# Clearing the raw weight blocks: other planning rules and new early due times

## The chip, the cores and the metric

The kernel runs on one core of one Trainium2 chip. The metric is the device time of one execution in microseconds (us). TensorE is called PE here, its weight loads PEld, VectorE DVE, ScalarE ACT, GpSimd POOL and the queue of transfers SP, as in the profile.

## The reference

The program chains three layers; everything is float32.

```python
# 1. a scan per batch (4) and head (8), 768 steps, state 48 x 48, complex decay
S_re, S_im = ar*S_re - ai*S_im + k[t] (x) v[t],  ar*S_im + ai*S_re
y[t] = q[t] @ S_re
# 2. x = y as 3072 tokens x 384;  rms norm, then a dense gated layer of width 1536
xn = x / sqrt(mean(x*x) + 1e-6) * rms_g
x  = (silu(xn @ w_gate) * (xn @ w_val)) @ w_out
# 3. 8 experts of width 1024, each token goes to its best one
e   = argmax(x @ w_gate2);  p = softmax(x @ w_gate2)[e]
out = p * (relu(x @ w1[e]) @ w2[e])
```

## The kernel before

The 3072 tokens are cut into 12 units of 256 tokens, each of two chunks of 128. A unit goes through three stages. `elem(u)` makes the decayed q and k of the scan with logarithms, exponentials, sines and running sums on ACT, DVE and POOL, and spreads them over partitions with transfers (tile QK). `attention(u)` calls `chunk` twice: scores, masking, products with v and with the state, and at the end the rms norm of each token (the root) and the split of the result into a high part xh and a low part xl. `dense(u)` runs 12 features of 128 columns: `stage1` is 18 matmuls, `stage2` 6, with a tanh and a few DVE steps between them. After unit 11 the experts follow.

The dense weights arrive as 64-bit floats, in 12 blocks: w00 to w03 of the gate, w10 to w13 of the value, wo0 to wo3 of the output. Features 0 to 2 need w00, w10 and wo0, features 3 to 5 need w01, w11 and wo1, and so on. `convert` turns a block into a high and a low part: three transfers into the block's own place, then in one of the raw buffers a memset (line 418), `top` (lines 395 and 397), `join` (line 401), `high` (lines 406 and 408), and `low` (line 411; for w00 and wo0 PE does it, lines 430 and 431, and ACT copies it, line 434). There are two raw buffers for all 12 blocks (NRAW=2), and `logit_columns` borrows them too. A raw buffer is given to a block when the first of its steps that touches it, the memset, is put in order.

The order of all instructions is made when the program is built, by `Plan.issue`. Each step has a list of engines with an estimated cost, the steps that it must follow (worked out from what it reads, r, and writes, w), and a due time. At each turn the planner finds the earliest time at which any step could begin, and among the steps that could begin then on that engine it takes the one with the smallest due time. So due times are priorities, and no real times. A step with `lock=True` is planned as using the port that DVE and POOL share: two locked steps on DVE or POOL are never planned at the same time. Each engine then runs its own list in that order, and waits only for the data that an instruction really touches.

A filler (`keep_warm`, line 1388) is planned on PE only where no other PE step could begin, and only up to W1=107.43 us of planned time; it multiplies a converted block into a buffer that nobody reads.

The due times that matter here: `due_moe(0, 3*g)` is 771.62 + 14.31 g, a block w{n}{g} is due at that + CG + C{n}{g}, a block wo{g} at that + CO + C2{g}. `due_elem(0)` is E0 + EU0 and `due_elem(1)` is 771.62 + E1 + EU1. `due_att(0)` is A0, with AC0 more for the second chunk; `due_att(1)` is 771.62 + A1 + AU1. Inside convert, the transfers of a block beyond the fifth in order of creation (w00, w10, wo0, w01, w11, wo1, w02, w12, wo2, w03, w13, wo3) are planned only after the `top` of the block five before it (AHEAD=5).

Of the kernel before, what the change touches and what calls it, by code (L numbers as in the profile page):

```python
# [27 lines left out]
          AF.Tanh: ("exp", "arctan", "sin")}  # L28
TABLE_LOAD = 1.3

TUNE = dict(T0=771.62, PER=649.53, FT=4.77, A0=-422.97, A1=-431.72, A2=-35.5, E0=-1137.13, E1=236.14, E2=1375.6,
            E3=785.18, CG=483.05, CO=263.88, LC=-203.35, NRAW=2, AHEAD=5, DH=547.2, FI=-16.42, RP=-1165.15, TOL=0,
            S2L=28.66, NS=3, NH=3, HOP=0.2, W1=107.43, ATP=2, PA0=0, PA1=0.08, PE0=0, PE1=0.24, RG=1, LB=-24.77,
            EB=-56.74, RB=6.57, HB=-60.28, MB=-8.8, TB=10.11, AX=1, EE=-12.66, EL=7.32, BEG=0.7, DL=2, FN=8,
            FF=15, LW=1, LO=1, C00=-926.96, C01=-266.61, C02=382.08, C03=-259.36, C10=-529.22, C11=-373.75, C12=-583.49,
            C13=1773.0, C20=-587.24, C21=781.76, C22=1957.05, C23=2500.91, C30=583.92, C31=-599.84, C32=-15.96, C33=-423.27,
            AU1=282.87, AU2=-63.05, AU3=-787.85, AU4=-777.43, EU0=224.54, EU1=294.16, EU2=16.71, EU3=-24.77,
            EU4=41.45, EU5=43.43, AC=73.5, AC0=4.7)
HOP = TUNE["HOP"]


# [92 lines left out]
class Plan:  # L134
# [5 lines left out]
    def add(self, engs, fn, r=(), w=(), due=0.0, table=None, lag=0.0, after=(), size=0, span=(0.0, math.inf), pull=0.0, lock=False):  # L140

        s = Step()
        s.size, s.span, s.pull, s.lock = size, span, pull, lock
        s.engs = [engs] if isinstance(engs, tuple) else engs
        s.fn, s.due, s.table, s.lag = fn, due, table, lag
        s.next, s.end, s.seq = [], None, len(self.steps)
        deps = {id(a): a for a in after}
        bufs = {}  # L150
        for writes, items in ((False, r), (True, w)):
            for x in items:
                b, part = x if isinstance(x, tuple) else (x, None)
                bufs[id(b)] = b
                for p, (wr, rd) in b.last.items():
                    if p == part or p is None or part is None:
                        for d in ([wr] if wr else []) + (rd if writes else []):
                            deps[id(d)] = d
        for writes, items in ((False, r), (True, w)):
            for x in items:  # L160
                b, part = x if isinstance(x, tuple) else (x, None)
                if writes:
                    if part is None:
                        b.last.clear()
                    b.last[part] = (s, [])
                else:
                    b.last.setdefault(part, (None, []))[1].append(s)
        deps.pop(id(s), None)
        s.bufs = list(bufs.values())
        for b in s.bufs:  # L170
            b.users += 1
        s.deps = list(deps.values())
        s.wait = len(s.deps)
        for d in s.deps:
            d.next.append(s)
        self.steps.append(s)
        return s
# [73 lines left out]
def kernel(ctx, tc, qT, kT, reT, imT, v, wg, wv, wo, rg, w2g, w1, w2, out):  # L251
    nc = tc.nc
    V, A, G, TE, SP = nc.vector, nc.scalar, nc.gpsimd, nc.tensor, nc.sync
# [123 lines left out]
    paces = []  # L377
# [3 lines left out]
    def convert(name, src, n, due, by_pe):  # L381

        place = Slots(left, name, [P, KD, n, 2], I32)
        st, raw, w = Buf(place), Buf(k_raw), Buf(place, shape=[P, KD, 2, n], dtype=F32R)
        N = KD * WB

        def halves():
            return st.t.rearrange("p k n t -> p k (n t)").bitcast(U16)

        def top(e):  # L390

            h = halves().bitcast(BF16).rearrange("p k (n t) -> p k n t", t=4)[:, :, 1:WB + 1, 0]
            o = raw.t.bitcast(F16).rearrange("p k (n t) -> p k n t", t=2)[:, :, :, 1]
            if e is A:
                e.activation(o, h, AF.Copy)
            else:
                e.tensor_scalar(out=o, in0=h, scalar1=1.0, scalar2=1.0, op0=ALU.mult, op1=ALU.mult)

        def join(e):
            ri = raw.t.bitcast(I32)  # L400
            e.scalar_tensor_tensor(out=ri, in0=st.t[:, :, :WB, 1], scalar=13, in1=ri,
                                   op0=ALU.logical_shift_right, op1=ALU.bitwise_or)

        def high(e):
            if e is A:
                e.activation(w.t[:, :, 0, :WB], raw.t, AF.Copy)
            else:
                e.tensor_scalar(out=w.t[:, :, 0, :WB], in0=raw.t, scalar1=1.0, scalar2=1.0, op0=ALU.mult, op1=ALU.mult)

        def low(e):  # L410
            e.tensor_tensor(out=w.t[:, :, 1, :WB], in0=raw.t, in1=w.t[:, :, 0, :WB], op=ALU.subtract)

        for k in range(KD):
            dma(lambda e, k=k: e.dma_start(halves()[:, k, 1:1 + 4 * WB], src[k * P:(k + 1) * P]),
                P * WB * 8, w=[(st, f"k{k}")], due=due, after=paces[-AHEAD:][:1] if len(paces) >= AHEAD else ())
        light = [(A, act(N)), (G, 0.08 + N * 1.04e-3), (V, dve(N / 2), TUNE["RB"])]
        pairs = [(st, f"k{k}") for k in range(KD)]
        add((G, 0.08 + N * 0.96e-3), lambda e: e.memset(raw.t, 0.0), w=[raw], due=due - 2, lock=True)
        paces.append(add(light, top, r=pairs, w=[raw], due=due, lock=True))
        add((V, dve(N)), join, r=pairs + [raw], w=[raw], due=due, lock=True)  # L420
        add(light, high, r=[raw], w=[(w, 0)], due=due, lock=True)
        if not by_pe:
            add([(G, pool2(N)), (V, dve(N), TUNE["LB"])], low, r=[raw, (w, 0)], w=[(w, 1)], due=due, lock=True)
            return w

        for k in range(KD):
            ps = bank(P, WB)

            def left_over(e, k=k, ps=ps):
                TE.matmul(ps.t, lhsT=ident, rhs=raw.t[:, k, :], start=True, stop=False)  # L430
                TE.matmul(ps.t, lhsT=NEGR.t, rhs=w.t[:, k, 0, :WB], start=False, stop=True)

            add((TE, mm(WB, 4) + mmr(WB)), left_over, r=[raw, (w, 0), NEGR], w=[ps], due=due)
            add((A, act(WB)), lambda e, k=k, ps=ps: e.activation(w.t[:, k, 1, :WB], ps.t, AF.Copy),
                r=[ps], w=[(w, f"l{k}")], due=due)
        return w
# [212 lines left out]
    def chunk(u, c, QK, vt, xh, xl, first, last):  # L649
# [143 lines left out]
                fn(e)  # L793

        if u < TUNE["RG"]:
            at((V, 0.19 * len(tiny_ops)), together, r=[rs], w=[rs])
        else:
            for fn in tiny_ops:
                at((V, 0.1), fn, r=[rs], w=[rs])
        at((A, act(DM)), lambda e: e.activation(wide(y.t), flat(), AF.Copy, scale=rs.t[:, 1:2]), r=[yp, rs], w=[y])  # L800
        xt = bank(P, KD, C)

# [754 lines left out]
```

## Time and profile before

| what | us |
|---|---|
| median of 3 runs | 936.32 (935.12 to 940.16) |
| the profiled execution: its time | 936.97 |
| the profiled execution: span, first to last instruction | 935.3 |
| PE busy | 896.5 (96% of the span) |
| DVE busy | 613.2 (66%) |
| ACT busy | 518.0 (55%) |
| POOL busy | 181.6 (19%) |
| mean granted clock of PE, as a share of full speed | 0.992 |

Busy times are those of the profiled execution. A busy PE need not do useful work: the filler counts as busy. Times of instructions count from the start of the span. A line number is that of the kernel before; the engine name stands ahead of it, and `out<-in` names what an instruction writes and reads.

### The profile page before, as it was taken

What the parts mean: (1) busy time and instruction counts of PE and PEld (TensorE: products, weight loads), DVE (VectorE), ACT (ScalarE), POOL (GpSimd) and SP (SyncE); (2) the same over time, 40 slices, a digit from 0 to 9 for tenths busy, and PEclk for the clock granted to TensorE, in tenths of its full rate; (3) what the DMA queues carried; (4) which work ended last, traced back from release to release, by engine and by line L of the source; (5) the groups of instructions that cost most, each with busy time, mean ns of one, the idle gap of its engine ahead of it and who ended that gap; (6) DMA issues with size and microseconds to landing.
All of it is one profiled execution on the core that took longest, in us unless ns stands there. A gap on an engine that the chain in (4) does not pass through costs nothing.

```text
span 935.3 us, 17743 instructions
## 1 busy us (share of the span) xinstructions
PE 896.5 (96%) x6747; PEld 863.5 (92%) x6747; DVE 613.2 (66%) x1528; ACT 518.0 (55%) x996; POOL 181.6 (19%) x226
## 2 busy tenths in 40 slices
PE   2699999999999999999999999999999999999996
PEld 2689999999999999999999999999989989999996
DVE  5699867778777768686868777546566642545510
ACT  7787876675655656655656565424426433544421
POOL 3232302010111010110201020101242532222121
PEclk9899999999999999999999999999999999999999
DMA  9955233423333140605050421102346753545200
GB/s 331 292 196 140 65 78 82 102 83 77 95 61 94 45 127 18 154 18 154 17 137 19 92 80 40 48 1 66 93 122 200 219 144 111 151 129 182 91 23 23
DMA packets 68363, 98.12 MB, mean 105 GB/s; under 512 B 16038, under 2 KB 49257, under 8 KB 68276
## 3 DMA queue, kind: packets, MB, share of 16 engines
q1 hardware_dynamic: 57316, 86.61, 32.9%
q0 software_dynamic: 10688, 9.95, 3.9%
q8 instruction: 54, 0.88, 0.4%
q10 hardware_dynamic: 272, 0.40, 0.1%
q14 instruction: 33, 0.27, 0.1%
HBM read 68.19 MB, written 10.15 MB: 84 GB/s over the span
## 4 chain that ended last, share of the span: by engine, by line
PE 68%; DVE 11%; issue 8%; DMA 5%; ACT 5%; POOL 2%; SPq 0%; POOLq 0%; DVEq 0%; ACTq 0%
PE m L850 25%; PE a L873 15%; PE a L1317 7%; PE m L1299 7%; PE t L680 4%; PE t L720 3%; DVE ee L541 2%; PE t L724 1%; DMA out_dram<-eo,idx 1%; PE t L698 1%; POOL out_dram L1325 1%; DMA QK<-qk 1%; DMA rawb<-in_w_dram 1%; DVE re L576 1%; DVE rs L785 1%
## 5 line engine op out<-in xcount | busy, mean ns | idle before, releaser
L850 PE MATMUL m<-xh,w 128*128 128x256 f32 x1728 | 276.6, 285 | 1.1 <-DVE s L862 0.6
L850 PEld LDWEIGHTS m<-xh,w 128*128 128x128 f32 x1728 | 234.6, 188 | 5.7 <-issue 3.4
L873 PE MATMUL a<-wo,hh 128*128 128x392 f32 (+1 forms) x576 | 151.8, 345 | 0.0
L850 PE MATMUL m<-xl,w 128*128 128x256 f32 x864 | 149.1, 281 | 0.0
L850 PEld LDWEIGHTS m<-xl,w 128*128 128x128 f32 x864 | 122.3, 188 | 0.0
L873 PEld LDWEIGHTS a<-wo,hh 128*128 128x128 f32 x576 | 100.5, 188 | 0.7 <-issue 0.7
L873 PE MATMUL a<-wo,hl 128*128 128x392 f32 (+1 forms) x288 | 98.3, 341 | 1.7 <-DVE hl L867 1.7
L865 ACT ACTIVATE hh<-s 128x256 fp32r<-128x256 f32 x144 | 59.5, 415 | 72.9 <-PE a L873 45.7
L857 ACT ACTIVATE s<-m 128x256 f32<-128x256 f32 x144 | 54.6, 380 | 77.8 <-PE m L850 40.1
L867 DVE TENSOR_TENSOR hl<-s,hh 128x256 fp32r<-128x256 f32 x144 | 66.6, 467 | 29.4 <-ACT hh L865 28.7
L859 DVE SCALAR_TENSOR_TENSOR s<-s,m 128x256 f32<-128x256 f32 x144 | 59.4, 413 | 21.3 <-ACT s L857 21.1
L1325 POOL DMA_INDIRECT out_dram<-eo,idx x28 | 37.2, 1330 | 157.7 <-ACT eo L1323 91.2
L1308 DVE SCALAR_TENSOR_TENSOR ehl<-m,ehh 128x384 fp32r<-128x384 f32 (+6 forms) x64 | 35.2, 555 | 44.6 <-ACT ehh L1306 44.0
L862 DVE SCALAR_TENSOR_TENSOR s<-s,m 128x256 f32<-128x256 f32 x144 | 59.6, 415 | 2.1
L1323 ACT ACTIVATE eo<-a,eg 114x384 f32<-114x384 f32 (+5 forms) x28 | 16.3, 582 | 74.9 <-PE a L1317 60.6
L873 PEld LDWEIGHTS a<-wo,hl 128*128 128x128 f32 x288 | 54.1, 188 | 2.3 <-DVE hl L867 2.3
L1306 ACT ACTIVATE ehh<-m 128x384 fp32r<-128x384 f32 (+6 forms) x64 | 31.2, 491 | 44.8 <-PE m L1299 41.7
L720 PE MATMUL t<-AK,vt 128*64 128x224 f32 (+3 forms) x384 | 49.6, 346 | 0.5 <-ACT raw L465 0.3
L680 PE MATMUL t<-QK 96*128 96x128 f32 x384 | 48.1, 276 | 0.3 <-DMA QK<-ee 0.3
L680 PEld LDWEIGHTS t<-QK 96*128 96x128 f32 x384 | 46.3, 192 | 1.3 <-issue 0.8
L948 POOL DMA_INDIRECT slots<-tid,sl x24 | 25.0, 1043 | 115.7 <-DVE cnt L943 111.8
L690 DVE TENSOR_TENSOR AK<-t,mask 128x512 f32<-128x512 f32 x40 | 26.9, 686 | 21.3 <-PE t L680 21.1
(290 smaller groups left out, 1853.0 us busy)
## 6 DMA issues: line engine op xcount, KB each, us to landing
rawb<-in_w_dram SPq DMA_DIRECT2D x21, 512.0 KB
rawb<-in_w_dram SPq DMA_DIRECT2D x28, 384.0 KB
QK<-qk SPq DMA_DIRECT2D x24, 290.2 KB
QK<-ee SPq DMA_DIRECT2D x24, 290.2 KB
re<-in_a_re_dram SPq DMA_DIRECT2D x12, 384.0 KB
im<-in_a_im_dram SPq DMA_DIRECT2D x12, 384.0 KB
qk<-in_q_dram SPq DMA_DIRECT2D x12, 384.0 KB
qk<-in_k_dram SPq DMA_DIRECT2D x12, 384.0 KB
```

What stands on the lines that cost most here:

```text
L680: TE.matmul(sc.t[:, i, :], lhsT=K(4 * g + i), rhs=Q(4 * g + i), start=True, stop=True)
L720: TE.matmul(yt.t[64 * n:64 * n + d, i, :n_], lhsT=vs[:, o:o + d], rhs=ak.t[:, 2 * i + n, :n_], start=True, stop=first)
L850: TE.matmul(ps.t[:, i, :], lhsT=W1[i, g].t[:, k, part, fs], rhs=x.t[:, k, :], start=(n == 0), stop=(n == 3 * KD - 1))
L857: add((A, act(U)), lambda e: e.activation(s.t, ps.t[:, 0, :], AF.Tanh, scale=0.5), r=[ps], w=[s], due=dh, table=AF.Tanh)
L859: add((V, dve(U)), lambda e: e.scalar_tensor_tensor(out=s.t, in0=s.t, scalar=1.0, in1=ps.t[:, 0, :], op0=ALU.add, op1=ALU.mult), r=[s, ps] ...
L862: add((V, dve(U)), lambda e: e.scalar_tensor_tensor(out=s.t, in0=s.t, scalar=0.5, in1=ps.t[:, 1, :], op0=ALU.mult, op1=ALU.mult), r=[s, ps ...
L865: add((A, act(U)), lambda e: e.activation(hh.t, s.t, AF.Copy), r=[s], w=[hh], due=dh)
L867: lambda e: e.tensor_tensor(out=hl.t, in0=s.t, in1=hh.t, op=ALU.subtract), r=[s, hh], w=[hl], due=dh, lock=True)
L873: TE.matmul(acc[t].t[:, :wide], lhsT=h.t[:, ts_], rhs=WO[g].t[:, k3, part, :wide], start=(f == 0 and n == 0), stop=(f == KF - 1 and n == 2))
L1299: TE.matmul(ps.t, lhsT=w.t[:, k, fs], rhs=y.t[:, k, :], start=(i == 0), stop=(i == 3 * KD - 1))
L1317: TE.matmul(po.t, lhsT=h.t[:, f, js], rhs=w.t[:, f, :], start=(f == 0 and i == 0), stop=(f == KF2 - 1 and i == 2))
L1325: add((G, 1.05), lambda e, o=o, j=j: e.indirect_dma_start(out=outs[(x + j) % len(outs)], out_offset=bass.IndirectOffsetOnAxis(ap=at(j), ax ...
```

## The change

Three things are edited. In `convert`, the memset of the raw buffer is no longer planned as a user of the shared port (`lock=True` is gone), and from the third block created on the planner must put it after the landing of the first of the block's three transfers (`r=pairs[:1]`). In `chunk`, the root is planned as a user of the shared port: all its instructions together for unit 0, the third one alone (line 785) for the other units, where each of them is a step of its own. And 33 constants of `TUNE` have new values, all of them due times; the numbers of buffers, the costs of the steps and what is computed stay.

```diff
--- before.py
+++ after.py
@@ -28,14 +28,14 @@
           AF.Tanh: ("exp", "arctan", "sin")}
 TABLE_LOAD = 1.3
 
-TUNE = dict(T0=771.62, PER=649.53, FT=4.77, A0=-422.97, A1=-431.72, A2=-35.5, E0=-1137.13, E1=236.14, E2=1375.6,
-            E3=785.18, CG=483.05, CO=263.88, LC=-203.35, NRAW=2, AHEAD=5, DH=547.2, FI=-16.42, RP=-1165.15, TOL=0,
+TUNE = dict(T0=771.62, PER=649.53, FT=4.77, A0=-208.38, A1=-534.31, A2=-35.5, E0=-913.69, E1=-117.22, E2=1310.91,
+            E3=785.18, CG=782.95, CO=398.33, LC=-594.82, NRAW=2, AHEAD=5, DH=547.2, FI=-16.42, RP=-439.99, TOL=0,
             S2L=28.66, NS=3, NH=3, HOP=0.2, W1=107.43, ATP=2, PA0=0, PA1=0.08, PE0=0, PE1=0.24, RG=1, LB=-24.77,
             EB=-56.74, RB=6.57, HB=-60.28, MB=-8.8, TB=10.11, AX=1, EE=-12.66, EL=7.32, BEG=0.7, DL=2, FN=8,
-            FF=15, LW=1, LO=1, C00=-926.96, C01=-266.61, C02=382.08, C03=-259.36, C10=-529.22, C11=-373.75, C12=-583.49,
-            C13=1773.0, C20=-587.24, C21=781.76, C22=1957.05, C23=2500.91, C30=583.92, C31=-599.84, C32=-15.96, C33=-423.27,
-            AU1=282.87, AU2=-63.05, AU3=-787.85, AU4=-777.43, EU0=224.54, EU1=294.16, EU2=16.71, EU3=-24.77,
-            EU4=41.45, EU5=43.43, AC=73.5, AC0=4.7)
+            FF=15, LW=1, LO=1, C00=-812.72, C01=-145.33, C02=-151.56, C03=-365.19, C10=-584.52, C11=-760.4, C12=-636.1,
+            C13=1713.57, C20=-538.76, C21=451.62, C22=2534.06, C23=2073.79, C30=271.16, C31=-476.58, C32=605.07, C33=-1214.84,
+            AU1=394.45, AU2=-1136.16, AU3=-1119.07, AU4=-815.88, EU0=32.96, EU1=286.28, EU2=521.23, EU3=-24.77,
+            EU4=41.45, EU5=43.43, AC=73.5, AC0=830.33)
 HOP = TUNE["HOP"]
 
 
@@ -415,7 +415,7 @@
                 P * WB * 8, w=[(st, f"k{k}")], due=due, after=paces[-AHEAD:][:1] if len(paces) >= AHEAD else ())
         light = [(A, act(N)), (G, 0.08 + N * 1.04e-3), (V, dve(N / 2), TUNE["RB"])]
         pairs = [(st, f"k{k}") for k in range(KD)]
-        add((G, 0.08 + N * 0.96e-3), lambda e: e.memset(raw.t, 0.0), w=[raw], due=due - 2, lock=True)
+        add((G, 0.08 + N * 0.96e-3), lambda e: e.memset(raw.t, 0.0), r=pairs[:1] if len(paces) > 1 else [], w=[raw], due=due - 2)
         paces.append(add(light, top, r=pairs, w=[raw], due=due, lock=True))
         add((V, dve(N)), join, r=pairs + [raw], w=[raw], due=due, lock=True)
         add(light, high, r=[raw], w=[(w, 0)], due=due, lock=True)
@@ -793,10 +793,10 @@
                 fn(e)
 
         if u < TUNE["RG"]:
-            at((V, 0.19 * len(tiny_ops)), together, r=[rs], w=[rs])
+            at((V, 0.19 * len(tiny_ops)), together, r=[rs], w=[rs], lock=True)
         else:
-            for fn in tiny_ops:
-                at((V, 0.1), fn, r=[rs], w=[rs])
+            for i, fn in enumerate(tiny_ops):
+                at((V, 0.1), fn, r=[rs], w=[rs], lock=i == 2)
         at((A, act(DM)), lambda e: e.activation(wide(y.t), flat(), AF.Copy, scale=rs.t[:, 1:2]), r=[yp, rs], w=[y])
         xt = bank(P, KD, C)
 
```

## Rows read from the trace of the kernel before

**Rows 1.** Three stretches: length, then busy PE, PEld, DVE, ACT, POOL, clock, DMA, GB/s.
```profile
0.00:60.00 60.00, 34.94 (x231) 28.79 (x232) 39.63 (x60) 46.37 (x66) 21.05 (x50) 0.94 0.95 313
60.00:84.00 24.00, 23.95 (x174) 23.68 (x173) 22.70 (x49) 19.82 (x32) 5.82 (x6) 1.00 0.25 83
84.00:130.00 46.00, 45.50 (x399) 42.83 (x398) 38.51 (x89) 37.23 (x68) 9.92 (x14) 1.00 0.32 79
```

**Rows 2.** Filler matmuls, groups by line: first 0 to 130, then 66 to 130.
```profile
L1388 PE MATMUL a<-w,identr 128*128 128x384 f32 x120 | 24.5, 358 | 5.3 <-ACT w L406 5.2
...
L1388 PE MATMUL a<-w,identr 128*128 128x384 f32 x28 | 5.5, 341 | 0.0
```

**Rows 3.** Chain that ended last, 0 to 130: start us, us, what.
```profile
30.57 8.35 DMA QK<-qk
...
38.93 3.08 DMA QK<-ee
...
52.54 1.27 DVE raw L401
...
54.09 1.69 DVE rs L785
...
57.12 1.27 DVE w L411
...
64.05 1.25 DVE raw L401
65.30 0.78 DVE xl L815 x3
...
76.09 6.40 PE m L850 x54
...
83.89 3.15 PE a L873 x18
```

**Rows 4.** Stretches of 10 us; the last two columns are DMA share and GB/s.
```profile
10.00:20.00 10.00, 3.27 (x6) 1.82 (x7) 8.17 (x16) 7.70 (x9) 1.27 (x1) 1.00 1.03 396
30.00:40.00 10.00, 4.79 (x26) 4.65 (x25) 6.77 (x6) 7.49 (x9) 1.18 (x2) 0.67 1.07 222
```

**Rows 5.** Timeline of POOL: start us, us, instruction, idle before and releaser.
```profile
20.94 1.15 POOL L418 MEMSET raw<- 128x1152 f32 x1 [0.27 <-PE t L430]
...
53.94 1.81 POOL L546 TENSOR_TENSOR im<-im,re 128x768 f32<-128x768 f32 x1 [2.30 <-ACT re L533]
```

**Rows 6.** Timeline of ACT, conversion steps of weight blocks.
```profile
30.79 1.50 ACT L395 ACTIVATE raw<-w 128x1152 f16<-128x1152 bf16 x1 [0.52 <-POOL raw L418]
32.88 1.50 ACT L395 ACTIVATE raw<-w 128x1152 f16<-128x1152 bf16 x1 [0.59 <-DMA w<-in_wv_dram]
...
35.72 2.20 ACT L406 ACTIVATE w<-raw 128x1152 fp32r<-128x1152 f32 x2
```

**Rows 7.** Timeline of DVE, 15 to 23 us.
```profile
15.32 1.36 DVE L401 SCALAR_TENSOR_TENSOR raw<-w,raw 128x1152 int32<-128x1152 int32 x1 [1.14 <-ACT raw L395]
16.60 2.03 DVE L554 TENSOR_TENSOR ee<-ee 128x256 f32<-128x256 f32 x3
...
20.51 0.58 DVE L585 TENSOR_SCALAR ta<-re 128x768 f32<-128x768 f32 x1
21.12 1.38 DVE L587 TENSOR_SCALAR ta<-ta 128x768 f32<-128x768 f32 x1
```

**Rows 8.** Line 785, the root: nanoseconds minimum, median, maximum of its instructions.
```profile
L785 DVE TENSOR_TENSOR rs<-magic,rs x24: 125/159/1805, 54.1 to 632.4; 128x1 int32<-128x1 int32 x24
```

**Rows 9.** DMA issues by line in 0 to 60: count, KB each.
```profile
w<-in_wg_dram SPq DMA_DIRECT2D x12, 384.0 KB
```

**Rows 10.** Timeline of DVE: first and last of unit 1's rest, 14 instructions.
```profile
66.19 1.09 DVE L554 TENSOR_TENSOR ee<-ee 128x256 f32<-128x256 f32 x3
...
82.86 1.82 DVE L613 TENSOR_TENSOR ee<-ee,re 128x768 f32<-128x768 f32 x2
```

**Rows 11.** The page's costliest groups: one of the dense stage's vector steps.
```profile
L859 DVE SCALAR_TENSOR_TENSOR s<-s,m 128x256 f32<-128x256 f32 x144 | 59.4, 413 | 21.3 <-ACT s L857 21.1
```

## Prediction

> **What bounds the kernel now.** I read the busy times by stretch first. From 84 us on PE hardly idles: 45.50 of 46 us are busy [rows 1]. In the first 60 us it is busy for only 34.94 us [rows 1], and the filler takes 24.5 us of the first 130, the last 5.5 of them after 66 us [rows 2]. So what the kernel loses it loses before about 84 us: some 25 us idle and 24.5 us of filler. The change alters nothing that PE must compute, so it can win or lose only by when useful PE work is ready there, and by new gaps later.
>
> The chain of waits says what ready depends on. The spread of unit 0 (QK) lands at 38.9 and 42.0 us [rows 3], behind a transfer queue that moves 396 GB/s between 10 and 20 us and is still full from 30 to 40 [rows 4]. From 52 to 66 us the chain runs through DVE: root, conversion steps of weight blocks, and the last piece of unit 0's xl, which ends at 66.08 [rows 3]. Dense work starts right after it. DVE is busy for 22.70 of the 24 us from 60 to 84 [rows 1]: it is the engine that unlocks PE work there.
>
> **The change part by part.**
>
> *The raw buffers.* Before, the memset has nothing to wait for, so the planner hands a free raw buffer to the block with the smallest due time, landed or not. The due times of before give 327.7 for w00, 448.3 for wo0, 699.8 for w12 and 725.5 for w10. The first two take the buffers at the start; w12 takes the next. The rows bear this out: a buffer is cleared at 20.94 [rows 5], and one of the two conversions that follow waits until 32.88 for weights of the value matrix [rows 6]. That buffer lies idle for 32.88 - 20.94 - 1.15 = 10.8 us. The new rule ends this. It adds no wait to the chip's POOL queue, since the memset reads nothing; it only moves the memset, and with it the choice of the block, down the order. w00 and w10 are the first two blocks created, are exempt, and take both buffers at the start; wo0 comes third, then w11 (808.5), and w01 (1423.6) if it has landed before w12 (947.1), which is fetched only after wo0's top. All of this fits into 24 to 42 us, where DVE is idle for about a third (6.77 of 10 busy from 30 to 40, [rows 4]). One whole conversion leaves the full stretch of 52 to 66. Its two DVE steps stand in the chain with 1.27 us each [rows 3]: 2.5 us less. Bounds: 0, if DVE takes other work ahead of xl instead, and 3.8, if all three such steps (1.27, 1.27, 1.25) go.
>
> *The root.* Line 785 takes 159 ns at the median and 1805 at most [rows 8]. Its long one in the chain, 1.69 us from 54.09 [rows 3], lies under a POOL multiplication of two tiles, 1.81 us from 53.94 [rows 5]. Planned apart, it costs 1.69 - 0.16 = 1.5 us less, on the path to xl. Bounds: 0, if real times shift the two together again, and 1.5. In later units DVE is not what PE waits for, so I count nothing there.
>
> *The order in elem(0).* Before, w00's join sits on DVE from 15.32, after 1.14 us of idle time, ahead of the subtraction that elem(0) needs next, which starts at 16.60 [rows 7]: 1.14 + 1.28 = 2.4 us lost. After, wo0 (631.2) is fetched ahead of w00 (741.9) but has no raw buffer, so nothing can be converted at that place until w00 lands one block later. A block is 3 x 384 KB [rows 9], 1.18 MB, or 3.0 us at 396 GB/s. The 2.4 us are won; but the spread then still meets the transfer queue, and w10 brings two DVE steps of its own into the tail of elem(0), where wo0 had one. I take half, 1.2 us, between 0 and 2.4.
>
> *The memset without the lock.* What a memset beside DVE costs is seen once: line 587 takes 1.38 us from 21.12, under the memset of 20.94 to 22.09, where the like line 585 took 0.58 [rows 5, 7], so 0.8 us. Without the lock the planner may put more of the 12 there. I take one on the path, 0.8 us more; bounds 0 and 4.8, for six.
>
> [...]
>
> *Due times.* The second chunk of unit 0 (622.0, before -418.3) now yields to the first but stays ahead of w00. elem(1) moves from 1301.9 to 940.7, ahead of w12, w10, w03, w01 and w02; w01 moves from 1002.4 to 1423.6. That shifts which PE work is unlocked first; by itself I count 0, and its price if it goes wrong is the third rival. On SP the spread keeps the smallest due time of what is ready (-648.4), so what counts is how many blocks were sent before it: five plus those whose gate has opened. I count seven, as before, so 0; bounds are one block either way, 3.0 us. Due times of units 2 to 5 and the late blocks (wo2 3732.6, last) reorder work where PE has other work ready: 0.
>
> **The sum**, against the profiled execution's own 936.97: -2.5 - 1.5 - 1.2 + 0.8 = -4.4, so 932.6. The median of the runs shown is 0.65 lower than that execution, so about 932 on its scale.
>
> **The rivals.**
> - *The filler goes as well.* If features 3 to 8 find weights and vector steps in time, the 5.5 us of filler after 66 us [rows 2] become useful work: 932 - 5.5 = 926.5. For it: with the idle buffer gone the right blocks (w01, w11) come by about 40 us. Against: part of that filler stands where PE waits for vector steps, which the change doesn't shorten.
> - *Hidden by the transfers.* One more block, w02 or w12, is sent ahead of the spread, 3.0 us; 932 + 3 = 935, no measurable change. For it: w10's top comes earlier and opens the gate of w02. Against: the spread is ready earlier too.
> - *w01 too late: slower.* Feature 3 needs w01, now due after elem(1), w12 and w10. If w01 falls behind the rest of elem(1) on DVE (9.7 us in 14 instructions, [rows 10]) and the 9 vector steps of features 0 to 2 (0.41 us each, [rows 11], 3.7 us), then at DVE's busy share of 22.70 of 24 it comes up 14.2 us after 66.1, and its own steps take 1.27 + 1.10 + 1.27 = 3.6 [rows 3, 6]: 83.9. Before, feature 3 starts at 76.1 [rows 3]; 7.8 us late, less 3.15 of stage 2 that PE can do meanwhile [rows 3], is 4.7; with w12 in front 2.5 more. 936.3 + 4.7 to 7.2 is 941 to 943.5; I take 943. It decides once w01 ends later than 76.1 + 3.15 = 79.3; from there each us costs one. Against: w01 is sent among the first five, and a raw buffer comes free while elem(1)'s inputs have not landed.
> - *Memsets collide.* Without the lock every memset ahead of the dense start can fall on a step like line 587. Six at 0.8 us are 4.8, four more than the 0.8 of the sum: 936. For it: the one case in the trace; against: most steps of DVE there have two inputs, and none of them is seen to stall under a memset. [...]
>
> **How the numbers follow.** Forecast 0.42, with its own range of 929 to 935; filler goes too 0.20; transfers hide it 0.20; w01 late 0.14; memsets 0.04. The likeliest is 932. Below 925 and above 942 I leave about one in ten each: 925 takes in the filler case with the root and buffer terms near their bounds, 942 half of the w01 case. A change under 0.5% (4.7 us) is about what a measurement of this kernel can't tell from none, so faster means below 931.6, slower above 941.0. Faster: the filler case and just over half of the forecast, 0.43. Slower: w01 late, 0.14. Same: the rest, 0.43.
>
> **What would show it.** In the new profile: no raw buffer cleared more than about 2 us before its top; w00 and w10 in the first two, five blocks done by about 42 us; no line 785 over 0.3 us in the first 66 us; the first dense matmul at 61 to 63 instead of 66; the spread landing by 42 or earlier; fewer than 120 filler matmuls. I am wrong if the spread lands later than 43, if PE idles or fills between features 2 and 3 for more than 5 us, or if new gaps come after 110 us, where I count none.

## The result: slower by 0.8%

| | before | after |
|---|---|---|
| median of 7 runs each, us | 936.38 | 944.77 (943.25 to 945.57) |
| ratio, 95% interval | 1 | 1.0081 (1.0064 to 1.0098) |
| span of the profiled execution, us | 935.3 | 943.1 |
| first dense matmul (L850), us | 66.4 | 69.9 |
| first expert product (L1299, xh with h1a), us | 683.8 | 688.4 |
| from there to the last L1317 with h2b, us | 243.3 | 246.5 |

The forecast of 932 and its range up to 942 missed. Of the 7.8 us by which the span grew, 4.6 come before the first expert product and 3.2 in the expert phase. The 4.6 are 3.4 us of later dense start, 1.0 us between the first and the last L850, and 0.2 us behind the last one.

**Start-up.** Busy times by stretch of the kernel after, columns as in [rows 1]:

```profile
0.00:60.00 60.00, 32.90 (x173) 27.96 (x173) 34.97 (x53) 43.03 (x58) 16.33 (x47) 0.94 0.89 293
...
37.00:43.00 6.00, 2.53 (x13) 2.08 (x12) 1.36 (x1) 1.31 (x4) 1.06 (x1) 0.86 1.04 267
43.00:60.00 17.00, 17.00 (x117) 15.40 (x115) 10.85 (x20) 13.85 (x21) 5.50 (x9) 0.85 0.65 231
```

The last two stretches of the kernel before:

```profile
37.00:43.00 6.00, 5.72 (x27) 5.56 (x28) 3.31 (x3) 3.72 (x6) 1.06 (x1) 0.73 1.01 205
43.00:60.00 17.00, 15.78 (x147) 13.08 (x146) 14.45 (x27) 14.68 (x25) 9.48 (x11) 1.00 0.89 323
```

Against [rows 1], DVE has done 34.97 instead of 39.63 us of work by 60 us, ACT 43.03 instead of 46.37. The prediction had one conversion more behind DVE by then. A busy time counts an instruction's whole length: 1.5 of the 4.7 us that DVE has less are the long line 785 of before (1.69 us, now 0.16), which is gone. In steps, one L411 (1.36 us), the three L815 of a chunk (0.82) and one each of L735, L756 and L704 (0.5 to 0.6) are missing by 60 us. From 37 to 43 us three engines idle together. Their timelines, kernel after, PE first, then ACT, DVE and POOL:

```profile
40.04 0.46 PE L680 MATMUL t<-QK 96*128 96x128 f32 x2 [2.72 <-DMA QK<-ee]
41.25 1.54 PE L680 MATMUL t<-QK 96*128 96x128 f32 x6 [0.75 <-DMA QK<-ee]
43.23 3.67 PE L680 MATMUL t<-QK 96*128 96x128 f32 x16
...
59.45 0.81 PE L430 MATMUL t<-raw,ident 128*128 128x384 f32 x2
...
42.83 0.60 ACT L684 ACTIVATE AK<-t 128x512 f32<-128x512 f32 x1 [4.69 <-PE t L680]
43.32 1.49 ACT L395 ACTIVATE raw<-w 128x1152 f16<-128x1152 bf16 x1
...
66.84 0.58 ACT L800 ACTIVATE y<-t,rs 128x384 f32<-128x384 f32 x1
...
43.47 0.56 DVE L704 COPY AK<-t 128x384 f32<-128x384 f32 x1 [4.70 <-PE t L698]
...
58.40 1.35 DVE L401 SCALAR_TENSOR_TENSOR raw<-w,raw 128x1152 int32<-128x1152 int32 x1
...
62.93 1.35 DVE L411 TENSOR_TENSOR w<-raw,w 128x1152 fp32r<-128x1152 f32 x1
...
68.75 1.35 DVE L401 SCALAR_TENSOR_TENSOR raw<-w,raw 128x1152 int32<-128x1152 int32 x1
...
75.63 2.01 DVE L411 TENSOR_TENSOR w<-raw,w 128x1152 fp32r<-128x1152 f32 x1
...
28.94 1.06 POOL L418 MEMSET raw<- 128x1152 f32 x1 [4.06 <-PE t L430]
...
38.83 1.06 POOL L418 MEMSET raw<- 128x1152 f32 x1 [5.62 <-DVE w L411]
...
60.32 1.06 POOL L418 MEMSET raw<- 128x1152 f32 x1 [3.95 <-PE t L430]
...
75.60 0.83 POOL L585 TENSOR_SCALAR ta<-re 128x768 f32<-128x768 f32 x1 [4.26 <-DVE re L576]
```

How to read it: PE waits for the spread (QK). On ACT the top of the next block (L395) stands right behind L684, which needs PE's scores; so that block's conversion waits for the spread too, although its buffer was cleared at 38.83. The other raw buffer is cleared for wo0 at 28.94, and wo0's third step on PE (L430) stands behind the scores and products of a whole chunk, at 59.45. Only then, at 60.32, is it cleared again: 31.4 us instead of the 10.8 us of idleness that the change was to cure. Before, ACT and DVE put conversions into the same wait [rows 6]. PE's idle time also brought its clock down: the 16 scores took 3.67 us, at a granted clock of 0.50 from 42 to 48 us, and 1.98 us at 1.00 in experiment 6, where PE has work in that wait.

Chain that ended last, kernel after, columns as in [rows 3]:

```profile
27.38 10.70 DMA QK<-qk
38.09 3.16 DMA QK<-ee
...
43.43 3.47 PE t L680 x16
...
47.54 1.77 PE a L1388 x8
...
50.97 1.61 PE a L1388 x8
...
54.58 1.44 PE a L1388 x8
...
57.70 1.59 PE a L1388 x8
...
61.77 1.61 PE a L1388 x8
...
64.78 1.47 PE a L1388 x8
...
66.87 1.46 PE a L1388 x8
...
75.72 1.92 DVE w L411
...
78.69 6.66 PE m L850 x54
```

The spread lands 0.8 us earlier than in [rows 3], though its transfers start 3.2 us earlier. Before, the chain lies mostly on DVE from 52 to 66 us, and one filler step stands in it between 42 and 66:

```profile
44.47 1.44 PE a L1388 x8
```

After, it lies on PE from 41.26 to 68.69 us. PE is busy for all of 43 to 60 us, and seven filler steps stand in the chain, 10.9 us together. The planner put them where it planned PE idle; on the chip some of the work behind them had its inputs earlier. The turn of y behind the last of the seven, for one, needs the y that L800 had written by 67.42, and that filler ends at 68.33. So the way to the dense start is no longer DVE's. What the filler on it costs no run here shows: experiments 13 to 16 cut only steps behind the dense start.

Behind the dense start DVE is in the chain again. Features 3 to 5 start at 78.69, after a gap of 1.12 us, behind the steps s of features 0 to 2, which stand behind L411. Line 411 took 2.01 us there, under POOL's L585, against 1.35 us for most others; that is 0.66 us. Against the start of the dense phase these features are not late: they follow it by 8.8 us, before by 9.5.

**Expert phase.** The first loads of expert weights for the second half (rawb), from the groups of L1088 by operation (count, ns minimum, median, maximum, first and last start), before:

```profile
L1088 SPq DMA_DIRECT2D rawb<-in_w_dram x21: 68/345/460, 685.1 to 859.6; - x21
```

After, with SP's wait of that line and PE's busy stretch that follows:

```profile
L1088 SPq DMA_DIRECT2D rawb<-in_w_dram x21: 332/346/1939, 699.1 to 867.4; - x21
...
SPq L1088 <- DVE w L1155: 4.9, 1, 4.9
...
710.00:720.00 10.00, 8.43 (x64) 7.76 (x62) 8.92 (x16) 7.98 (x16) 1.54 (x1) 1.00 0.67 182
720.00:730.00 10.00, 9.25 (x50) 8.63 (x50) 5.12 (x10) 3.55 (x5) 2.30 (x2) 1.00 0.61 189
```

They go out 14.0 us later, after a wait of 4.9 us for L1155, a DVE step of `join_late`, and one of 4.6 for L1175, a PE step of it; that function borrows the memory of w10 in both kernels. PE then idles for 1.57 and 0.75 us, where before it idles for none.

### The profile page after: what moved, and what is told of

It is laid out like the page before. It is cut to its first block, busy times and chain, and to the rows that moved or that the text cites. A ratio compares the mean times of both kernels' runs of the same rounds, so it can differ in the third digit from the quotient of the medians.

```text
span 943.1 us, 17747 instructions
## 1 busy us (share of the span) xinstructions
PE 900.3 (95%) x6747; PEld 866.1 (92%) x6747; DVE 616.4 (65%) x1537; ACT 515.8 (55%) x994; POOL 167.3 (18%) x219
## 4 chain that ended last, share of the span: by engine, by line
PE 73%; issue 7%; DMA 7%; DVE 6%; ACT 4%; POOL 1%; SPq 0%; POOLq 0%; ACTq 0%; DVEq 0%
PE m L850 29%; PE a L873 15%; PE a L1317 6%; PE m L1299 5%; PE t L680 5%; PE t L720 4%; DMA rawb<-in_w_dram 3%; PE t L724 2%; PE a L1388 2%; DMA out_dram<-eo,idx 1%; PE t L698 1%; DMA QK<-qk 1%; POOL out_dram L1325 1%; PE t L805 1%; PE t L765 1%
## 5 line engine op out<-in xcount | busy, mean ns | idle before, releaser
L850 PE MATMUL m<-xh,w 128*128 128x256 f32 x1728 | 275.0, 284 | 1.7 <-DVE s L862 1.7
L850 PEld LDWEIGHTS m<-xh,w 128*128 128x128 f32 x1728 | 233.7, 188 | 5.0 <-issue 2.7
L873 PE MATMUL a<-wo,hh 128*128 128x392 f32 (+1 forms) x576 | 152.7, 346 | 0.0
L850 PE MATMUL m<-xl,w 128*128 128x256 f32 x864 | 149.4, 281 | 0.0
L850 PEld LDWEIGHTS m<-xl,w 128*128 128x128 f32 x864 | 122.2, 188 | 0.4 <-DVE xl L815 0.2
L873 PEld LDWEIGHTS a<-wo,hh 128*128 128x128 f32 x576 | 100.7, 189 | 1.4 <-issue 1.1
L873 PE MATMUL a<-wo,hl 128*128 128x392 f32 (+1 forms) x288 | 98.4, 342 | 1.9 <-DVE hl L867 1.9
L862 DVE SCALAR_TENSOR_TENSOR s<-s,m 128x256 f32<-128x256 f32 x144 | 59.7, 416 | 2.3
L873 PEld LDWEIGHTS a<-wo,hl 128*128 128x128 f32 x288 | 54.1, 188 | 2.2 <-DVE hl L867 2.2
L680 PE MATMUL t<-QK 96*128 96x128 f32 x384 | 50.9, 285 | 3.5 <-DMA QK<-ee 3.5
L680 PEld LDWEIGHTS t<-QK 96*128 96x128 f32 x384 | 48.4, 199 | 5.3 <-issue 4.2
```

The costliest lines, as they stand in the source:

```text
L680: TE.matmul(sc.t[:, i, :], lhsT=K(4 * g + i), rhs=Q(4 * g + i), start=True, stop=True)
L850: TE.matmul(ps.t[:, i, :], lhsT=W1[i, g].t[:, k, part, fs], rhs=x.t[:, k, :], start=(n == 0), stop=(n == 3 * KD - 1))
L862: add((V, dve(U)), lambda e: e.scalar_tensor_tensor(out=s.t, in0=s.t, scalar=0.5, in1=ps.t[:, 1, :], op0=ALU.mult, op1=ALU.mult), r=[s, ps ...
L873: TE.matmul(acc[t].t[:, :wide], lhsT=h.t[:, ts_], rhs=WO[g].t[:, k3, part, :wide], start=(f == 0 and n == 0), stop=(f == KF - 1 and n == 2))
```

## The experiments

Ratios are to the kernel before, on the same chip, with their 95% intervals. "The changed kernel" is the one after. The times of experiments 2 to 7, 9, 11 and 12 lie outside the ranges expected, those of 5, 6, 11 and 12 by less than 2 us.

**1. Other memory for join_late.**

```diff
-            buf, pn = Buf(W1[1, 0].slots, ...
+            buf, pn = Buf(W1[1, 3].slots, ...
```

> The changed kernel with one edit: join_late borrows the memory of w13 and no longer that of w10. Theory (memory): after the change rawb lies over w10, because the blocks are placed in the order of their transfers, so the first load of expert 1's weights waits for the last readers of the borrowed w10, at 699.1 us where it was 685.1. Then this kernel loads them about 9 us earlier, and about 3 us come off: 941.5 to 942 where the changed kernel has 944.8; the dense end (688.6 us) stays. Rival (transfers): the loads are late only because the dense phase ends late, so nothing moves: 944.8.

941.71 us, 1.0051 (1.0029 to 1.0073). The loads of rawb go out at once again, and from 710 to 720 us PE is busy for all 10.00:

```profile
L1088 SPq DMA_DIRECT2D rawb<-in_w_dram x21: 112/345/791, 689.2 to 863.6; - x21
```

The expert phase is back at 243.3 us. So some 3 us of the loss come from the place in memory (3.2 in the traces, 2.8 by the ratios, whose intervals overlap a little): rawb now shares it with w10, whose memory the join uses late.

**2. Twenty fillers ahead of the first scores.**

```diff
...
+                for _ in range(20 if warm else 0):
+                    TE.matmul(fill.t, lhsT=identr, rhs=W1[0, 0].t[:, 0, 0, :WB], start=True, stop=True)
...
```

> The changed kernel with 20 filler matmuls (3.4 us) put on PE straight ahead of unit 0's first scores, where PE stands idle from 37.3 to 40.0 us. Theory (clock): the idle stretch is followed by half the granted clock from about 41 to 48 us, on unit 0's scores, which the first dense matmul waits for. With PE busy the clock stays at 1.0, the 16 score matmuls that took 3.67 us take 1.8, the first dense matmul comes at 66.5 to 67.5 instead of 69.9, and the time is 941 to 942.5. Rival (vector work): from 41 to 70 us the chain is set by DVE and ACT, so the clock rises but the first dense matmul stays at 69 to 70 and the time at 944 to 945.

968.33 us, 1.0332 (dense start 99.2). It tells nothing of the clock: those matmuls write the filler's buffer, so the planner put one group's scores behind all filler, at 67.9 us. Experiments 5 and 6 do it in the bank of the scores.

**3 and 4. The halves of the change.** 3 has the rules of before and the new constants, 4 the new rules and the constants of before.

> The rules of before (memset locked and free to come early, root not locked) with the new due times. Theory (due times): the loss comes with the due times, through the order of the transfers (memory, clock), so this is as slow as the changed kernel or slower, 943 to 950. Rival (rules): the new memset rule costs the time, so this is at 936 to 939.

962.12 us, 1.0265 (1.024 to 1.0291); dense start 78.5, end 711.2.

> The new rules (memset after its weights and not locked, root locked) with the due times of before. Theory (due times): the rules by themselves free the raw buffer that lay idle and separate the root from the multiplication; with the old order of transfers neither memory nor clock changes, 933 to 937. Rival (rules): the new memset rule costs the time, 941 to 946.

950.77 us, 1.015 (1.0124 to 1.0176); dense start 81.5, end 700.8. Each half is worse than the whole: either one replans the start-up, and the constants make good part of what the rules cost. The memset's rule has no run of its own.

**5 and 6. Small matmuls ahead of the first scores,** 32 and then 48, in the scores' own bank, so that the plan stays.

```diff
-                for i in range(4):
+                for i in range(-48 if u + c + g == 0 else 0, 4):
...
```

For i below 0 the product is that of the identity with itself.

> The changed kernel with 32 small matmuls on the identity (128 columns, about 3.5 us) straight ahead of unit 0's first scores; they write where the scores write afterwards, and every other instruction keeps its place. Theory (clock): PE no longer stands idle from 37.3 to 40.0 us, the granted clock stays at 1.0 through 41 to 48 us where it was 0.5, the first dense matmul comes at 66.5 to 68 instead of 69.9, and the time is 941.5 to 943 (944.8 without). Rival (vector work): DVE and ACT set the chain to the first dense matmul, so that the clock rises and the first dense matmul stays at 69.5 to 70: 944 to 945.

941.02 us, 1.0029 (1.0008 to 1.0049). With 32 a gap of 0.99 us is left, and the clock falls all the same:

```profile
40.00:42.00 2.00, 1.01 (x9) 0.85 (x9) 0.00 (x0) 0.00 (x0) 0.00 (x0) 1.00 1.00 225
42.00:48.00 6.00, 6.00 (x32) 6.00 (x33) 1.91 (x2) 2.92 (x4) 1.38 (x5) 0.55 1.02 362
```

The dense phase starts at 70.5 and ends at 689.0, so what this run gains lies in the expert phase (243.4 us) and not in the clock here: the loads of rawb go out as late as in the changed kernel (699.6), but PE idles for only 1.3 us behind them, and a stretch at half clock that comes and goes (last section) is absent: the clock is 1.00 from 760 to 780 us.

> As the run with 32 small matmuls ahead of unit 0's first scores, but with 48 (5.3 us at the 0.11 us each that the 32 took), so that PE has work until the last of the spread has landed at about 41.9 us; there a gap of 1.0 us was left and the clock fell all the same. Theory (clock): without a gap the granted clock stays at 1.0 through 42 to 50 us, the 16 score matmuls take 1.8 instead of 3.7 us, the first dense matmul comes at 66.5 to 68.5 instead of 69.9, and the dense phase ends 1.5 to 3 us earlier: 941.5 to 943. Rival (vector work): the clock stays up and the first dense matmul doesn't move: 944 to 945.5.

940.45 us, 1.004 (1.0028 to 1.0052). Now the clock stays. First the changed kernel's stretch, then this one's, and its 16 scores:

```profile
42.00:48.00 6.00, 6.00 (x30) 6.00 (x30) 1.92 (x2) 3.01 (x5) 1.47 (x5) 0.50 1.00 337
```

```profile
42.00:48.00 6.00, 6.00 (x53) 5.62 (x54) 2.42 (x3) 4.26 (x6) 2.14 (x5) 1.00 1.03 364
...
43.73 1.98 PE L680 MATMUL t<-QK 96*128 96x128 f32 x16
```

The dense phase starts 1.9 us earlier (68.0), and its last L850 comes 2.0 us earlier (675.8 instead of 677.9). So the clock's price at the start is carried through the dense phase. The first expert product comes only 0.3 us earlier (688.1): behind the last L850 PE waits 2.07 us for DVE, as it waited 1.87 us in the changed kernel, but here half clock follows:

```profile
682.53 0.48 PE L873 MATMUL a<-wo,hl 128*128 128x392 f32 x1 [2.07 <-DVE hl L867]
...
684.00:686.00 2.00, 2.00 (x7) 2.00 (x7) 1.70 (x5) 1.15 (x2) 0.00 (x0) 0.50 0.06 2
```

That stretch takes 1.7 us back. The same order in other traces bears out the gain: with the 48 matmuls (experiments 6, 12, 15 and 16) the dense phase starts at 67.6 to 68.7 and the last L850 comes at 675.2 to 676.8; without them (the changed kernel and experiment 1) at 69.9 and 70.1, and at 677.9 and 677.6. The rest of its gain lies in the expert phase (243.2 us), whose order this edit leaves alone: 1.7 us are the stretch at half clock after 765 us told of in the last section (here 1.00 from 765 to 785); the loads of rawb still go out late (698.8), but PE idles for only 0.97 us behind them.

**7. An earlier due time for wo0** (C20 from -538.76 to -1500).

> The changed kernel with wo0 due at -330 instead of 631, ahead of unit 0's chunks. Theory (raw buffer held by wo0): in the changed kernel the last of wo0's three steps on PE stands behind the first chunk, so its raw buffer is held from 28.9 to 60.3 us; with the step ahead of the chunk the buffer is free by about 40, and the next conversions come 15 us earlier; the filler at 86 to 90.5 us shrinks by half or more: 940 to 943. Rival (clock or vector work): the dense start at 69.9 sets the end, and earlier conversions are not waited for: 944 to 946.

963.44 us, 1.0278 (1.0246 to 1.0311); dense start 73.5. The whole block moved, and the order behind it.

**8. A later due time for the first logit columns** (C30 from 271.16 to 975.35).

> The changed kernel with the first group of logit columns due at 1801.7, as before the change, instead of 1097.5. Theory (raw buffer held by the logit columns): they hold a raw buffer from about 77 to 87 us, ahead of w01, w02 and wo1, and the conversions from 85 us on wait for it; due later, they leave it to the conversions: 941 to 943.5. Rival: the buffer is not what the conversions wait for, DVE is: 944 to 947.

943.2 us, 1.0058 (1.0036 to 1.008); dense end unchanged at 688.4. The time lies in the theory's range, but the gain is in the expert phase (244.1 us), where again no half clock follows 765 us (1.00 from 760 to 780). The logit columns' use of a raw buffer is not what is lost.

**9. The second chunk's due time as before** (AC0 4.7).

> The changed kernel with the due time of unit 0's second chunk at that of the first plus 4.7, as before, instead of 830.3 later. Theory (clock and memory): the order of the two chunks is not what costs the time; the first dense matmul stays within 2 us of 69.9 and the time within 942 to 948. Rival (chunks): the second chunk, put behind the first, sets the late dense start; interleaved, the dense start comes 3 us earlier or more: 939 to 941.5.

959.51 us, 1.0243 (1.0223 to 1.0262); dense start 70.3, but gaps, and a clock of 0.83 from 136 to 140 us and 0.50 from 140 to 152.

**10. The root's rule alone,** in the kernel before.

```diff
-            at((V, 0.19 * len(tiny_ops)), together, r=[rs], w=[rs])
+            at((V, 0.19 * len(tiny_ops)), together, r=[rs], w=[rs], lock=True)
...
-            for fn in tiny_ops:
-                at((V, 0.1), fn, r=[rs], w=[rs])
+            for i, fn in enumerate(tiny_ops):
+                at((V, 0.1), fn, r=[rs], w=[rs], lock=i == 2)
```

> The kernel before with the new rule for the root alone (planned as a user of the shared port). Theory: the 1.69 us of line 785 in the chain to unit 0's xl go, and little else moves: 934.5 to 936.5 (936.2 without). Rival (a moved step reorders the rest): the dense start moves by more than 3 us either way: under 933 or over 939.

945.98 us, 1.0084 (1.0055 to 1.0113). The dense phase starts at 64.7, 1.7 us earlier than in the trace of before (0.9 us earlier than in experiments 13 and 14, which have the order of before up to there), about what the prediction's step has (1.5), and ends 8.4 us later:

```profile
128.07 0.55 PE L805 MATMUL t<-ident,y 128*128 128x128 f32 x3 [1.10 <-ACT y L800]
...
134.00:140.00 6.00, 6.00 (x33) 6.00 (x33) 3.19 (x10) 1.55 (x4) 2.87 (x2) 0.50 0.63 122
```

PE waits 1.1 us for ACT and then runs at half clock for some 14 us, which do the work of about 7 (an estimate from the two clocks). That alone is more than was won; which unit's locked root brings the wait isn't separated here.

**11. The same with 20 small matmuls at that wait.**

> The kernel before with the root's new rule alone, and 20 small matmuls (2.2 us) on the identity where PE waits 1.1 us at 127.0 us (the turn of y of unit 1's second chunk); every other instruction keeps its place. With the root's rule alone the first dense matmul came 1.7 us earlier than before, and the time was 8 us longer; after that wait the clock was at 0.5 from 128.5 to 142.5. Theory (clock): the short wait costs its time by the clock; with PE kept busy the clock stays at 1.0, some 6 to 7 us come back, and the time is 934 to 939. Rival (order): the time is lost by the new order of vector work, with or without the clock: 943 to 947.

948.58 us, 1.0121 (1.0099 to 1.0143). The clock fell still, to 0.50 from 130 to 146 us, so it doesn't settle the price of the clock there.

**12. Experiments 1 and 6 together.**

> The changed kernel with both cures: join_late borrows w13's memory, and 48 small matmuls stand ahead of unit 0's first scores. Theory: memory and clock add up, 3 + 2 to 3 us: 938.5 to 940, which leaves 2 to 4 us to the kernel before, for the raw buffers that wo0 and the logit columns hold. Rival: the clock is worth nothing, 941.5 to 942.

940.1 us, 1.0029 (1.0016 to 1.0041): rawb at 688.3, expert phase 242.9, dense start 68.7, dense end 688.6. With experiment 5 it has the lowest ratio of the changed kernels, still above 1. The gains don't add: from experiment 6 to this one the median falls by 0.35 us only. In this profile another wait of 1.2 us has come in at 710 to 720 us, for a gather of tokens; experiment 16, with the same two repairs, has no gap of that size there. What is left against before lies ahead of the first expert product, by phase (us):

| | before | after | 6 | 12 |
|---|---|---|---|---|
| first L850 | 66.4 | 69.9 | 68.0 | 68.7 |
| from there to the last L850 | 607.0 | 608.0 | 607.8 | 607.9 |
| from there to the first expert product | 10.4 | 10.6 | 12.3 | 12.1 |

The last row is longer in 6 and 12 by half clock behind a wait of 2.07 and 1.85 us for DVE (a clock of 0.83 from 680 to 690 us in both); in the changed kernel the clock stays at 1.00 behind such a wait of 1.87, and the row is 10.6.

**13 to 16. Filler after the dense start.** PE runs 15 filler steps of 8 matmuls in both kernels. Of the last three, some are cut here to one matmul each; the order of all else stays.

```diff
-            add(..., lambda e, w=w, k=k: keep_warm(e, w, k), ...
+            add(..., lambda e, w=w, k=k, n=1 if i == 14 else 8: keep_warm(e, w, k, n), ...
```

In the kernel before, the last one, and then all three:

> The kernel before, with the last of its 15 filler steps (the 8 matmuls that stand at 82.32 us, ahead of the stage 2 of features 0 to 2) cut to one matmul; order, plan and all else stay. Filler as a cost: the hh and hl that this stage 2 reads are written by 77.7 us, so PE has work there; 7 matmuls of 0.18 us go, the dense stage ends 1.2 us earlier, 935.2 on the scale of 936.4. Filler as a cover: something else (a bank or a block) is awaited there, a gap of about 1 us opens, and the end stays at 683.8 us or, if PE then runs at half clock, comes some 3 us or more later.

934.65 us, 0.9986 (0.9971 to 1.0001): not told apart from before by its time. In the trace, the first to the last L850 take 606.0 us instead of 607.0, as filler as a cost would have it; two traces of one dense order (the changed kernel and experiment 1) differ by 0.5 us in this.

> The kernel before, with the last three of its filler steps (16 matmuls at 73.02 us, 8 at 82.32) cut to one matmul each. At 73 to 74.7 us PE then has nothing to do, since the banks m come free only with the steps s of L862 from 74.3 us on. Filler as a cost: 1.2 us from the last step, and about 1.2 us more at 73 us, where the first bank is free 1.2 us ahead of the filler's end: 934.0. Filler as a cover of the clock: the gap of about 1.5 us at 73 us is followed by a stretch at half clock of 7 us or more, as in the other runs with a gap of about 1 us: 937 to 941.

935.32 us, 0.9997 (0.9982 to 1.0012), again 606.0 us. Feature 3 comes 1.2 us sooner behind the dense start, but PE then waits 0.97 us for DVE (L862) ahead of feature 6: as a whole the 16 at 73 us are a cover. The gap of 1.12 us that opens there leaves the clock at 1.00, against the second theory.

In experiment 12's kernel, the first, and then all three:

> The changed kernel with the other memory for the join and 48 small matmuls ahead of the first scores (median 940.1), and with one filler step cut to a single matmul: the 8 that stand at 84.89 us, between L460 and L466. Filler as a cost: L466 waits behind them, L473 on DVE waits for L466, and L859 and L862 of features 3 to 5 stand behind L473; all of them come 1.1 us earlier, and so does the feature after the other 16 fillers: 939.0, dense end 687.5. Filler as a cover: those features wait for something else, and the time stays at 940.1.

940.99 us, 1.0054 (1.0035 to 1.0073).

> The same kernel with all three filler steps after the dense start (24 matmuls at 84.89 to 89.3 us) cut to one matmul each. Filler as a cost: 4 us more PE time is there, but the feature behind waits for L862 of features 3 to 5, about 3 us later; 1.1 to 1.5 us less, 938.8, with PE idle for some 2.5 us at 85 to 88. Filler as a cover of the clock: that gap is followed by half clock, and the time is 941 or more.

939.47 us, 1.0051 (1.003 to 1.0072). Neither gains: by their ratios they are no faster than experiment 12 (1.0029), and the half clock of the second theory did not come. With the filler gone PE simply waits:

```profile
87.72 0.63 PE L850 MATMUL m<-xh,w 128*128 128x256 f32 x3 [2.82 <-DVE s L862]
...
84.00:88.00 4.00, 1.17 (x6) 0.64 (x6) 4.00 (x10) 3.34 (x5) 1.06 (x1) 1.00 0.47 98
88.00:92.00 4.00, 4.00 (x33) 4.00 (x33) 4.00 (x5) 2.21 (x2) 0.00 (x0) 1.00 1.04 194
```

DVE is busy for all of 84 to 88 us. So in the changed kernel these three steps cover waits for DVE. With them cut in both kernels, feature 6 starts 20.1 us after the dense start here and 19.3 in experiment 14; that 0.8 us is what DVE's lag costs up to there.

**17 and 18. wo0's PE steps ahead of everything** (it was the third that stood late), on top of experiment 12, and alone.

```diff
+            soon = due if len(paces) < 3 else -2000.0
-            add((TE, mm(WB, 4) + mmr(WB)), left_over, r=[raw, (w, 0), NEGR], w=[ps], due=due)
+            add((TE, mm(WB, 4) + mmr(WB)), left_over, r=[raw, (w, 0), NEGR], w=[ps], due=soon)
...
```

> The changed kernel with the other memory for the join and the 48 small matmuls (median 940.1), and with one due time more: the third PE step of wo0 (and its copy on ACT) comes ahead of everything, so PE does it at about 37 us instead of 59 and wo0's raw buffer is free some 22 us earlier. The held raw buffer as the cause of what the dense phase still loses: the seventh and eighth join end at most 65 and 72 us instead of 68.9 and 81.3, DVE idles less than 12 us from 30 to 60 us, the dense phase ends 2 to 4 us earlier, 936 to 938. Any change of order costs: the order behind it is planned anew, as in the runs with one changed due time, and the time is 942 or more though the buffer is free.

959.24 us, 1.0247 (1.0225 to 1.0269); dense start about 74.5. The clearing of raw buffers (POOL's timeline):

```profile
42.98 1.05 POOL L418 MEMSET raw<- 128x1152 f32 x1
64.91 1.06 POOL L418 MEMSET raw<- 128x1152 f32 x1 [9.83 <-DVE rs L783]
```

> The changed kernel with that one due time alone (median 944.8 without it): neither the other memory nor the small matmuls. Held raw buffer as the cause: 2 to 4 us less, 941 to 943, and the loads of rawb still wait, about 3 us; the step of PE at about 37 us also fills a part of PE's idle time there. Any change of order costs: 947 or more.

961.92 us, 1.0277 (1.0258 to 1.0297). wo0's buffer is free at 43 us in both, but two other blocks now hold both buffers until 64.91 (65.87 in experiment 18), because the steps L411 that would free them were planned late. DVE's work from 30 to 60 us didn't rise (16.38 us in experiment 17, 17.45 in experiment 12). So wo0's held buffer isn't shown to be the cause of the backlog; freeing it moved the hold elsewhere.

## Why the prediction was wrong

- **The raw buffers, the largest term (-2.5), is the step that failed.** It said: "One whole conversion leaves the full stretch of 52 to 66." None did: after, two joins and one L411 lie between 52 us and the dense start (58.40, 62.93, 68.75), as before (52.54, 57.12, 64.05 in [rows 3]), and by 42 us four joins were done in either kernel, not five. The rule did take away the clearing of a buffer for a block that had not landed. But wo0, third as foretold, then held its buffer for 31.4 us, and the next block's top stood behind L684 on ACT. From 37 to 60 us DVE was busy for 12.2 instead of 17.8 us, 1.5 of the difference being the long line 785. I costed the choice of the block and not when its last step would be ordered: nothing in the sum asked which steps share a queue with those that wait for the spread. And this gain, like the root's, was priced on DVE as the way to the dense start, while after the change that way lies on PE from 41.26 to 68.69 us. What the memset's rule would cost by itself isn't measured.
- **The root (-1.5): right where it stands, wrong as a whole.** The long line 785 is gone (0.16 us at 55.71, against 1.69 in [rows 3]), and experiment 10 starts the dense phase 0.9 to 1.7 us earlier. It also makes the kernel 0.84% slower: far behind it a wait of 1.1 us is followed by some 14 us at half clock. The prediction counted nothing for the later units.
- **The order in elem(0) (-1.2): half right, too large.** The spread is sent 3.2 us earlier, 26.56 instead of 29.75, and lands 0.8 us earlier. Seven blocks go out ahead of it in both kernels, as counted, so it is not the rival "hidden by the transfers", which had one block more, but the step's own reserve, that the spread still meets the transfer queue. It could have been sent earlier still (next point).
- **The memset without the lock (+0.8):** up to 90 us no clearing lies beside a slowed step; the price came from other pairs, which are locked in the plan and still met on the chip. One is L411 under L585, 0.66 us. The larger one stands ahead of the spread: two L608 take 3.05 us under POOL's top (L397), 1.83 before. The port that the lock stands for is an assumption of the plan and shown by no run; the trace shows these longer DVE steps beside POOL's.

```profile
23.45 3.05 DVE L608 TENSOR_TENSOR qk<-ee,ta 128x768 f32<-128x768 f32 x2 [0.85 <-ACT ta L597]
...
23.38 1.50 POOL L397 TENSOR_SCALAR raw<-w 128x1152 f16<-128x1152 bf16 x1 [4.11 <-DMA w<-in_wv_dram]
```

- **Due times (0): the second failed step.** I asked only which PE work they unlock. They also order the weight transfers, and with them where the blocks lie; the join's memory and rawb then overlapped, some 3 us by experiment 1 (less in experiments 5, 6 and 8, where PE idles 1.0 to 1.5 us behind the late loads instead of 2.3), in a phase where I had costed nothing.
- **The clock wasn't in the sum.** PE's idle time before the first scores took 1.9 us from the dense start and 2.0 us at the last L850 (experiment 6). In the kernel before, the like wait, 5.21 us, lay ahead of filler (L1388 at 36.91), and from 42 to 48 us, with the scores, its clock was 1.00.
- **"Fewer than 120 filler matmuls" didn't come true:** both kernels run all 15 steps. That is the plan's doing: experiment 3's kernel runs 48 matmuls in 6 steps. After 66 us the kernel after runs 42 of them instead of 28 [rows 2].
- **The slow rival named a time of 943 for another reason.** Feature 3 waited 1.12 us for the steps s on DVE, not for w01, and the 5 us of idling or filler between features 2 and 3 that I had named didn't come.

Of the 7.8 us, some 3 are the place in memory (experiment 1) and 1.9 the clock ahead of the scores (experiment 6). What stays open are some 2 to 3 us: in experiments 6 and 12 the dense phase starts 1.6 and 2.3 us later than before and takes 0.8 us longer up to its last L850. Part of that is within what one order varies from trace to trace (the dense start by 0.9 us in the three traces with the order of before, by 1.1 in the four with the 48 matmuls). One rival is untested, and it stands where the loss is: the filler steps that lie in the chain to the dense start. The filler behind it isn't the loss (experiments 15 and 16). Nor is it settled which order would give the rest back: each earlier due time that I tried (7, 9, 17, 18) cost more than it freed.

## What to carry to other kernels

A step taken off an engine is worth its time only while the way to the goal lies on that engine; read the chain again after the change. Where a planner sets the order, a small rule is no local edit: price it by what stands behind each waiting instruction on every in-order queue until its result is used, above all a shared buffer's last reader. Ask of each reordered transfer where its data will lie and who reuses that place, hundreds of us later too. And look in the new plan for stretches in which all engines wait for one transfer; what was planned into that wait before is the first thing to be lost.

## What was not expected of the hardware

A short gap was followed by half clock at some places and not at others. It was after 0.99 us (experiment 5) and 1.10 us (experiment 10, half clock for some 14 us); it was not after 2.82 us of experiment 16 or 1.12 of experiment 14, both between dense matmuls. At one and the same L873, behind the last L850, a wait of 1.85 us was followed by half clock in experiment 12 (0.83 from 680 to 690 us), and one of 1.87 us by a clock of 1.00 in the changed kernel. In the expert phase it differs between kernels whose order there is alike. Before, and then experiment 13:

```profile
765.00:770.00 5.00, 3.22 (x16) 2.58 (x14) 1.51 (x3) 2.17 (x4) 0.00 (x0) 1.00 0.23 91
770.00:775.00 5.00, 4.96 (x16) 4.41 (x17) 1.70 (x3) 0.55 (x1) 0.00 (x0) 0.66 0.41 106
```

```profile
765.00:770.00 5.00, 3.61 (x18) 2.96 (x17) 2.58 (x4) 2.54 (x5) 0.00 (x0) 1.00 0.44 120
770.00:775.00 5.00, 5.00 (x30) 4.84 (x29) 3.24 (x4) 3.57 (x5) 0.00 (x0) 1.00 0.03 6
```

Idle for 1.78 and then 1.39 us, with clocks of 0.66 and 1.00 behind it. The 1.7 us that this makes are there in the traces of before, after and experiments 1 and 16, and not in those of 5, 6, 8, 12, 13, 14 and 15: they come and go, and no edit here is shown to set them. The length of a gap alone doesn't tell whether the clock falls.
